# The opening of a fused attention and gated-MLP kernel: tile order, instruction order on four engines, and weight loads in row parts

## Chip, cores, metric

One core of a Trainium2 chip. The metric is the device time in microseconds of one execution; a profile's span is that of TensorE's and the other engines' records, 1.6 to 2.0 us shorter.

## The reference

```python
def _layernorm(x, eps=1e-5):            # over the last axis
    return (x - mean(x)) / sqrt(var(x) + eps)

# A_x [1, 2048, 1024], A_wqkv [1024, 3072], A_wo [1024, 1024], B_w1/B_w3 [1024, 3584], B_w2 [3584, 1024], all bf16
xn = _layernorm(A_x)
q, k, v = split(xn @ A_wqkv)            # 32 heads of 32
s = dilated_window_attention(q, k, v) @ A_wo     # 8 keys per query, 2 apart
g = silu((silu(xn @ B_w1) * (xn @ B_w3)) @ B_w2)
out = A_x + s * g
```

## The kernel before

The rows of x come in four chunks of 512, each of four tiles of 128 rows. Every projection is done with a seven-product (Strassen-like) scheme in bf16 and fp16: "sums" of weight blocks and of x blocks on VectorE, products on TensorE, copies out of the PSUM, the buffer that TensorE writes to, on ScalarE. Below, x1 and x2 are chunks 1 and 2; the "x1 sums" are the sums of blocks of x that chunks 0 and 1 make together. Chunk 0's q, k and v start with two plain products (called `first` and `second` below) that need no sums; the other products of the seven follow when the sums with chunk 1 are there. The parts that the change touches:

```python
x_load(0)                                     # four loads of 256 KB
wq0 = qkv_load(0, 0, slot(2, (4, D)))         # one load of 1 MB: half of the rows of the q weights
wq1 = qkv_load(0, 1, slot(6, (4, D)))
wk0 = qkv_load(1, 0, slot(8, (4, D)))
x_load(1)
...
ln_dve(0, [0])        # statistics and normalising on VectorE, the root on ScalarE
ln_act(0, [1])        # tile 1: two accumulating passes, root and normalising on ScalarE
ln_dve(0, [2])
ln_dve(0, [3])

def p1(g, th):        # first q product, output pair g, half th of the 512 columns
    ...
    act_copy(snap[g][:, :, cols], pf[g][:, :, cols])

spin_in(0, 0, 5)      # idle-filling matmuls: no result, they keep TensorE busy
tpose(0, 0); tpose(0, 1)                      # tile 0: 4 + 4 transposes on TensorE
untp(0, 0, dve_copy); untp(0, 1, sc_copy)     # PSUM -> SBUF
tpose(1, 0); tpose(1, 1)
untp(1, 0, sc_copy); untp(1, 1, sc_copy)
tpose(2, 0); tpose(2, 1)
untp(2, 0, dve_copy)
p1(0, 0)
tpose(3, 0); tpose(3, 1)
...
p1(1, 0); p1(0, 1); p1(1, 1)
...                                           # chunk 1: statistics, 3 tiles transposed by DMA, 1 on TensorE
for t, ... in (q, k, v):
    first_two(...)                            # first and second product of q, k, v
qkv_sums(wq0, wq1, sq)
xn_sums(xT[:, 0], xT[:, 1], b12, xT[:, 2], xs)    # four sums of x blocks, each of 512 columns
qkv_sums(wk0, wk1, sk)
qkv_seven(0, 0, wq0, wq1, sq, None, snap[0:2])
```

A scheduler places the instructions on each engine; `hp()` raises a priority and `tc.issue_after` pins one instruction behind another.

## Time and profile before

| | before |
|---|---|
| time, median of the runs | 725.17 us (724.62 to 725.53, 4 runs) |
| span of the profiled run | 723.4 us |
| TensorE busy | 710.8 us, 98% |
| first q product | 11.42 us |
| seven-product part starts | 33.18 us |

The prediction shows the lines. How to read them: a line of the timeline gives start and duration of a run of like instructions, and in brackets the idle time ahead of it with what ended that. The waits view sums those idle times. For a kernel whose TensorE never idles after its first product, the place to look is the time at which that product starts, and afterwards any mark in the stream (the start of k, of v, of the seven-product part): a mark that moves by 1 us moves the end by 1 us, unless a new hole eats it.

### The profile page before, as it was taken

To read this page: it belongs to the slowest core of one execution; us is meant where nothing else is said; L and a number is where in the kernel's file an instruction comes from. 1 tells how busy PE (TensorE), PEld (TensorE's weight loads), DVE (VectorE), ACT (ScalarE), POOL (GpSimd) and SP (SyncE) were. 2 spreads that over 40 slices of the span, in tenths; PEclk is the share of its full clock that TensorE was granted. 3 is DMA by queue.
4 is the path that set the end of the run, shared out by engine and by line. 5 is a ranking of instruction groups with operands and counts; after the bars stand their busy time and mean duration, and the time that the engine had idled before them with its cause. 6 is when DMAs were issued, how large, how long until landed. Compare 5 with 4: busy or idle time off the path is not lost.

```text
span 723.4 us, 8708 instructions
## 1 busy us (share of the span) xinstructions
PE 710.8 (98%) x3299; PEld 345.6 (48%) x3353; DVE 623.7 (86%) x687; ACT 314.8 (44%) x329; POOL 96.1 (13%) x162
## 2 busy tenths in 40 slices
PE   8999999999999999999999999999999999999996
PEld 5655666554444444444444444444444444444442
DVE  6995879779879878978999999969859989998974
ACT  5754334356545456554545312024454573020233
POOL 0011100011310000233111000000435005000011
PEclk9999999999999999999999999999999999999999
DMA  9966156868755523568756637459799544563615
GB/s 326 278 151 163 58 199 213 270 233 256 230 170 176 174 88 117 160 198 259 247 172 215 204 131 243 150 194 377 172 282 326 156 139 149 163 207 126 211 26 108
DMA packets 119049, 139.51 MB, mean 193 GB/s; under 512 B 17504, under 2 KB 94304, under 8 KB 118368
## 3 DMA queue, kind: packets, MB, share of 16 engines
q1 hardware_dynamic: 104464, 97.01, 43.8%
q0 software_dynamic: 14544, 41.95, 18.5%
q8 instruction: 26, 0.43, 0.2%
q14 instruction: 15, 0.12, 0.1%
HBM read 96.21 MB, written 38.80 MB: 187 GB/s over the span
## 4 chain that ended last, share of the span: by engine, by line
PE 95%; ACT 2%; DVE 1%; issue 1%; DMA 1%; SPq 0%; DVEq 0%; ACTq 0%
PE bm L149 20%; PE am L149 13%; PE em L149 13%; PE db L149 10%; PE bq L149 9%; PE de L149 7%; PE da L149 7%; PE eq L149 5%; PE aq L149 3%; PE af L149 2%; PE wb L149 2%; PE we L149 2%; PE wa L149 2%; DMA wring<-in_A_x_dram 1%; PE af L1022 1%
## 5 line engine op out<-in xcount | busy, mean ns | idle before, releaser
L149 PEld LDWEIGHTS <-wring 128*128 128x128 f16 (+1 forms) x1808 | 185.7, 103 | 205.4 <-issue 1.6
L149 PEld LDWEIGHTS <-h_sb 128*128 128x128 f16 (+1 forms) x1056 | 109.6, 104 | 118.2 <-issue 0.8
L149 PE MATMUL bm<-xs,wring 128*128 128x512 f16 x504 | 117.4, 379 | 0.2
L149 PE MATMUL am<-xT,wring 128*128 128x512 bf16 x322 | 79.0, 379 | 0.8
L149 PE MATMUL db<-wring,h_sb 128*128 128x512 f16 x336 | 73.2, 379 | 0.0
L475 DVE TENSOR_TENSOR BC<-Ep,vT 128x2048 bf16<-128x2048 bf16 x56 | 66.7, 1219 | 0.1
L420 DVE TENSOR_TENSOR pt<-qt,kT 128x4096 bf16<-128x4096 bf16 x24 | 55.0, 2291 | 0.6
L658 DVE TENSOR_TENSOR um<-em,um 128x1024 f32<-128x1024 f32 x28 | 34.2, 1223 | 21.0 <-PE em L149 13.3
L660 ACT ACTIVATE g<-um 128x1024 bf16<-128x1024 f32 x28 | 29.6, 1057 | 48.6 <-DVE um L658 48.6
L149 PE MATMUL da<-wring,h_sb 128*128 128x512 bf16 x219 | 48.7, 379 | 0.3
L461 POOL DMA_DIRECT2D Ep<-pb x64 | 38.0, 601 | 52.2 <-DVE pb L457 46.4
L149 PE MATMUL bm<-h_sb,wring 128*128 128x512 f16 x168 | 39.7, 379 | 0.0
L149 PE MATMUL em<-xs,wring 128*128 128x512 f16 x168 | 39.7, 379 | 0.0
L149 PE MATMUL em<-xT,wring 128*128 128x512 bf16 x161 | 39.2, 379 | 0.3
L485 DVE TENSOR_TENSOR oT<-oT,BC 128x2048 bf16<-128x2048 bf16 x32 | 39.0, 1220 | 0.3
L159 ACT COPY bm<-am 128x1024 f32<-128x1024 f32 x28 | 27.9, 998 | 25.9 <-PE am L149 25.9
L159 ACT COPY pm<-em 128x1024 f32<-128x1024 f32 x28 | 28.4, 1013 | 20.1 <-PE em L149 20.1
L159 ACT COPY um<-bm 128x1024 f32<-128x1024 f32 x28 | 28.4, 1013 | 18.9 <-PE bm L149 18.9
L679 ACT CAST g<-bm 128x1024 bf16<-128x1024 f32 x28 | 28.3, 1010 | 17.4 <-PE bm L149 17.4
L673 DVE TENSOR_TENSOR h_sb<-bm,pm 128x1024 bf16<-128x1024 f32 x21 | 25.6, 1218 | 5.1 <-PE bm L149 5.0
L422 DVE TENSOR_TENSOR pt<-pt 128x2048 bf16<-128x2048 bf16 x24 | 29.3, 1222 | 0.4
L483 DVE TENSOR_TENSOR BC<-BC 128x2048 bf16<-128x2048 bf16 x24 | 29.3, 1221 | 0.4
(202 smaller groups left out, 994.0 us busy)
## 6 DMA issues: line engine op xcount, KB each, us to landing
wring<-in_B_w_dram SPq DMA_DIRECT2D x61, 512.0 KB, 4.5
wring<-t_dram SPq DMA_DIRECT2D x16, 512.0 KB, 3.8
t_dram<-wring POOLq DMA_DIRECT2D x14, 512.0 KB, 4.0
wring<-t_dram SPq DMA_DIRECT2D x16, 384.0 KB, 4.9
wring<-in_B_w_dram SPq DMA_DIRECT2D x12, 384.0 KB, 4.4
wring<-in_A_x_dram SPq DMA_DIRECT2D x16, 256.0 KB, 5.6
Ep<-pb POOLq DMA_DIRECT2D x64, 64.0 KB, 5.4
wring<-in_A_wo_dram SPq DMA_DIRECT2D x8, 512.0 KB, 5.3
```

What stands on the lines that cost most here:

```text
L149: anchor["pe"] = nc.tensor.matmul(ps, lhsT=lhs[k], rhs=rhs[k], start=(first and k == 0), stop=(k == n - 1), skip_group_check=not first,)
L159: nc.scalar.copy(out=out_, in_=in_)
L420: nc.vector.tensor_mul(p_t[:], q[:], kT[:, :, o:o + CH])
L422: nc.vector.tensor_add(p_t[:, 0:4, :], p_t[:, 0:4, :], p_t[:, 4:8, :])
L461: nc.gpsimd.dma_start(out=pr[c][r:P:NR, :, sq * P:(sq + 1) * P], in_=pb[sq * 32:(sq + 1) * 32, :, :])
L475: nc.vector.tensor_mul(dst, E[:, w, :].unsqueeze(1).to_broadcast([P, n, CH]), vT[:, js, o:o + CH])
L483: nc.vector.tensor_add(B, B, C)
L485: nc.vector.tensor_add(A, A, B if w0 else C)
L658: v = nc.vector.tensor_add(su2[:], pe[:], su2[:])
L660: nc.scalar.activation(out=hl["g"][:, :, CH:], in_=su2[:], func=ACTF.Silu)
L673: anchor["v"] = nc.vector.tensor_add(h[:, :, CH:], pb[:], sp5[:])
L679: nc.scalar.copy(out=hl["g"][:, :, 0:CH], in_=pb[:])
```

## The change

Its intent: start the stream of products earlier. Tiles 0 and 1 are normalised first, both by VectorE; the first q products run on tiles 0 and 1 before tiles 2 and 3 are transposed; the q weights come in quarters of 256 KB, taken in the order of their rows; the second half of the k weights and both halves of v come in pieces of 512 KB; and the instructions of the opening on VectorE and ScalarE, and those of TensorE from the k products on, are pinned each behind the one before it. Of chunk 1, TensorE now transposes tile 2, the DMA the other three (before: TensorE tile 3). The first two x1 sums are done for three of four column tiles first, so that they need not wait for the last tile.

```diff
-    wq0 = qkv_load(0, 0, slot(2, (4, D)))
-    wq1 = qkv_load(0, 1, slot(6, (4, D)))
+    wq0 = qkv_load(0, 0, slot(2, (4, D)), 4)
+    wq1 = qkv_load(0, 1, slot(6, (4, D)), 4)
...
-    ln_dve(0, [0])
-    ln_act(0, [1])
-    ln_dve(0, [2])
-    ln_dve(0, [3])
+    st_half(0, 0); st_half(0, 1); st_half(1, 0)
+    st_end(0); root(0)
+    st_half(1, 1); st_end(1); root(1)
+    apply(0); apply(1)
...
+    spin(tpb[0], SP0)              # SP0, SP1 = 2, 1
     tpose(0, 0); tpose(0, 1)
+    with behind("t"):
+        spin(tpb[2], SP1)
     tpose(1, 0); tpose(1, 1)
+    untp(0, 0, sc_copy); untp(1, 0, sc_copy); untp(0, 1, sc_copy)
...                                 # statistics, roots, apply of tiles 2 and 3
+    one = [(k,) for k in range(KH)]
+    p12(0, 0, one, (0,))           # first product, columns 0-255, a weight row part at a time
+    p12(0, 0, one, (1,))
     tpose(2, 0); tpose(2, 1); tpose(3, 0); tpose(3, 1)
...
+    p12(1, 0, one)                 # second product, columns 0-255
+    p12(0, 1, one, (0,)); p12(0, 1, one, (1,))
+    p12(1, 1, [range(KH)])
...                                 # q sums, statistics of chunk 1, k and v products, one by one in order
-    xn_sums(xT[:, 0], xT[:, 1], b12, xT[:, 2], xs)
+    for n, cols in enumerate((slice(0, 3 * P), slice(3 * P, CH))):
+        s_k[n]()
+        dve(nc.vector.tensor_sub, xs[:, 0, :, cols], b12[:, :, cols], xT[:, 0, :, cols])
+        dve(nc.vector.tensor_sub, xs[:, 1, :, cols], xT[:, 2, :, cols], xs[:, 0, :, cols])
+    dve(nc.vector.tensor_sub, xs[:, 2], xT[:, 2], b12)
+    dve(nc.vector.tensor_sub, xs[:, 3], xT[:, 1], xs[:, 1])
```

More of the change, by code (lines that the diff above doesn't have):

```diff
@@ L115 @@
     SLOT = KH * CH
+    SP0, SP1 = 2, 1
     wring = keep.tile([P, 10, SLOT], BF16, name="wring")
@@ L148, in mm @@
         for k in range(n):
-            anchor["pe"] = nc.tensor.matmul(
-                ps, lhsT=lhs[k], rhs=rhs[k], start=(first and k == 0),
-                stop=(k == n - 1), skip_group_check=not first,
-            )
+            with behind("pe") if "open" in anchor else nullcontext():
+                anchor["pe"] = nc.tensor.matmul(
+                    ps, lhsT=lhs[k], rhs=rhs[k], start=(first and k == 0),
+                    stop=(k == n - 1), skip_group_check=not first,
+                )
     def a4(name, shape=(2, CH), dt=FP32):
@@ L165, in flush @@
             pend.pop(0)()
-    def first_two(key, A, b11, b21, snap, e11, mid=lambda: None, pa=None):
-        have, pa = pa, pa or []
-        for g in range(2):
-            if have is None:
-                pa.append(bank2(f"a{key}{g}"))
-                for i in I:
-                    mm(pa[g][:, i], A[g][0][i], b11, True)
-                act_copy(snap[g], pa[g][:])
-        mid()
-        for g in range(2):
-            for i in I:
-                mm(pa[g][:, i], A[g][1][i], b21, False)
-            e11[g](pa[g])
     def seven(key, A, B, e11, e12, e22, e21, snap=None):
@@ L240, in behind, with act, dve @@
         return tc.issue_after(anchor[key].ins) if key in anchor else nullcontext()
+    def act(f, **kw):
+        with hp(), behind("a"):
+            anchor["a"] = f(**kw)
+    def dve(f, *args, **kw):
+        with behind("ln") if "open" in anchor else nullcontext():
+            r = f(*args, **kw)
+        if "open" in anchor:
+            anchor["ln"] = r
     def ln_dve(c, sts):
@@ L307, with qkv_sums @@
     B0 = B_of(xT[:, 0], xT[:, 1], xT[:, 2], xs)
-    def qkv_sums(w0, w1_, st, again=False):
+    def qkv_sums(w0, w1_, st, again=False, parts=False):
         lo = lambda w: w.rearrange("p k (c two j) -> p k c two j", two=2, j=4)[:, :, :, 0]
@@ L323, in qkv_sums @@
             return
-        nc.vector.tensor_add(s1, a21, a22)
-        nc.vector.tensor_sub(s2, s1, a11)
-        nc.vector.tensor_sub(s4, a12, s2)
-        nc.vector.tensor_sub(s3, a11, a21)
+        parts_ = [
+            lambda: dve(nc.vector.tensor_add, s1, a21, a22), lambda: dve(nc.vector.tensor_sub, s2, s1, a11),
+            lambda: dve(nc.vector.tensor_sub, s4, a12, s2), lambda: dve(nc.vector.tensor_sub, s3, a11, a21),
+        ]
         pace["owed"] += 4.5
+        if parts:
+            return parts_
+        for f in parts_:
+            f()
     def qkv_A(w0, w1_, st, g):
@@ L333, in qkv_A @@
         v3 = w0.bitcast(FP16).rearrange("p k (c two j) -> p k two j c", two=2, j=4)
-        sv = [s.rearrange("p k (c j) -> p k j c", j=4) for s in st]
+        sv = [s.rearrange("p k (c j) -> p k j c", j=4) for s in st or ()]
         pick = lambda v, h: [[v[:, k, h, 2 * g + i, :] for k in range(KH)] for i in I]
         sp = lambda q: [[sv[q][:, k, 2 * g + i, :] for k in range(KH)] for i in I]
+        if st is None:
+            return pick(v0, 0), pick(v1, 0)
         return pick(v0, 0), pick(v1, 0), pick(v1, 1), sp(0), sp(1), pick(v3, 1), sp(2)
@@ L375, in qkv_seven, with qkv_load @@
                 mid(g)
-    def qkv_load(t, h, wt):
-        anchor["wq"] = nc.sync.dma_start(out=wt, in_=wqkv_r[:, h * 4:(h + 1) * 4, t * D:(t + 1) * D])
+    def qkv_load(t, h, wt, n=1):
+        for k in range(0, 4, 4 // n):
+            k1 = k + 4 // n
+            anchor["wq"] = nc.sync.dma_start(out=wt[:, k:k1], in_=wqkv_r[:, h * 4 + k:h * 4 + k1, t * D:(t + 1) * D])
         return wt
@@ L984 @@
     wve = [att_tile((4, D), BF16, f"wve{h}") for h in I]
+    wk1 = qkv_load(1, 1, rows(0, 4).rearrange("p (k n) -> p k n", k=4), 2)
+    for h in I:
+        qkv_load(2, h, wve[h][:], 2)
     vsn = att_tile((2, 2, CH), FP32, "vsn")
@@ L991, in tpose @@
     def tpose(st, a):
-        key = a, st // 2
-        if key not in tpb:
-            tpb[key] = bank2(f"tp{a}{st // 2}")
-        tp = tpb[key]
+        if st not in tpb:
+            tpb[st] = bank2(f"tp{st}")
         for k in range(KH):
-            nc.tensor.matmul(
-                tp[:, st % 2, k * P:(k + 1) * P], lhsT=xt[0][:, st, (a * KH + k) * P:(a * KH + k + 1) * P], rhs=ident[:],
+            anchor["t"] = nc.tensor.matmul(
+                tpb[st][:, a, k * P:(k + 1) * P], lhsT=xt[0][:, st, (a * KH + k) * P:(a * KH + k + 1) * P], rhs=ident[:],
                 start=(k == 0), stop=(k == KH - 1), skip_group_check=True,
@@ L1002, in untp @@
     def untp(st, a, eng):
-        with hp():
-            r = eng(out=xT[:, a, :, st * P:(st + 1) * P], in_=tpb[a, st // 2][:, st % 2].rearrange("p (k t) -> p k t", k=KH))
-        if eng == dve_copy:
-            anchor["x"] = r
+        with hp(), behind("a" if eng == sc_copy else "ln"):
+            r = eng(out=xT[:, a, :, st * P:(st + 1) * P], in_=tpb[st][:, a].rearrange("p (k t) -> p k t", k=KH))
+        anchor["ln" if eng == dve_copy else "a"] = r
     dve_copy, sc_copy = nc.vector.tensor_copy, nc.scalar.copy
-    ln_dve(0, [0])
@@ L1010 @@
-    ln_act(0, [1])
-    ln_dve(0, [2])
-    ln_dve(0, [3])
-    pf = {}
-    def p1(g, th):
-        if g not in pf:
-            pf[g] = bank2(f"af0{g}")
-        cols = slice(th * 2 * P, (th + 1) * 2 * P)
-        w = wq0.rearrange("p k (c two j) -> p k two j c", two=2, j=4)
-        for i in I:
-            for k in range(KH):
-                nc.tensor.matmul(
-                    pf[g][:, i, cols], lhsT=w[:, k, 0, 2 * g + i, :], rhs=xT[:, 0, k, cols],
-                    start=(k == 0 and th == 0), stop=(k == KH - 1), skip_group_check=True,
-                )
-        act_copy(snap[g][:, :, cols], pf[g][:, :, cols])
@@ L1028, in spin_in, with st_half @@
-    def spin_in(st, a, n):
-        tpb[a, st // 2] = bank2(f"tp{a}{st // 2}")
-        spin(tpb[a, st // 2], n)
-    spin_in(0, 0, 5)
+    st0 = rows(10, 1, FP32)[:, 0:15 * NST].rearrange("p (a b) -> p a b", b=NST)
+    stats = st0[:, 0:12].rearrange("p a b -> p (a b)").rearrange("p (s h d) -> p s h d", s=NST, h=2)
+    mv = st0[:, 12:14].rearrange("p a b -> p (a b)").rearrange("p (s d) -> p s d", s=NST)
+    rstd = st0[:, 14]
+    def st_half(st, h, c=0):
+        dve(nc.vector.bn_stats, out=stats[:, st, h, :], in_=xt[c][:, st, h * CH:(h + 1) * CH])
@@ new lines, in st_end, with root, apply @@
+    def st_end(st):
+        dve(nc.vector.bn_aggr, out=mv[:, st, :], in_=stats[:, st])
+    def root(st):
+        act(nc.scalar.activation, out=rstd[:, st:st + 1], in_=mv[:, st, 1:2], func=ACTF.Sqrt, bias=eps_t[:], scale=1.0)
+    def apply(st, c=0):
+        r = rstd[:, st:st + 1]
+        dve(nc.vector.reciprocal, out=r, in_=r)
+        dve(
+            nc.vector.tensor_scalar, out=xt[c][:, st, :], in0=xt[c][:, st, :], scalar1=mv[:, st, 0:1], scalar2=r,
+            op0=ALU.subtract, op1=ALU.mult,
+        )
@@ new lines, with p12 @@
+    pf = {}
+    wqs = [w.rearrange("p k (c two j) -> p k two j c", two=2, j=4)[:, :, 0] for w in (wq0, wq1)]
+    def p12(n, th, ks, gs=range(2), save=True):
+        for g in gs:
+            if g not in pf:
+                pf[g] = bank2(f"af0{g}")
+        cols = slice(th * 2 * P, (th + 1) * 2 * P)
+        for kh in ks:
+            for g in gs:
+                for i in I:
+                    for k in kh:
+                        nc.tensor.matmul(
+                            pf[g][:, i, cols], lhsT=wqs[n][:, k, 2 * g + i, :], rhs=xT[:, n, k, cols],
+                            start=(n == 0 and k == 0 and th == 0), stop=(k == KH - 1), skip_group_check=True,
+                        )
+        if n == 0:
+            for g in gs:
+                act(nc.scalar.copy, out=snap[g][:, :, cols], in_=pf[g][:, :, cols])
@@ L1033 @@
+    anchor["open"] = True
+    st_half(0, 0)
+    st_half(0, 1)
+    st_half(1, 0)
+    st_end(0)
+    root(0)
+    st_half(1, 1)
+    st_end(1)
+    root(1)
+    apply(0)
+    apply(1)
+    tpb[0], tpb[1], tpb[2] = [bank2(f"tp{k}") for k in range(3)]
+    spin(tpb[0], SP0)
     tpose(0, 0)
     tpose(0, 1)
-    untp(0, 0, dve_copy)
-    untp(0, 1, sc_copy)
+    with behind("t"):
+        spin(tpb[2], SP1)
     tpose(1, 0)
     tpose(1, 1)
+    untp(0, 0, sc_copy)
     untp(1, 0, sc_copy)
-    untp(1, 1, sc_copy)
+    untp(0, 1, sc_copy)
@@ L1041 @@
+    st_half(2, 0)
+    st_half(2, 1)
+    st_half(3, 0)
+    st_end(2)
+    root(2)
+    st_half(3, 1)
+    st_end(3)
+    untp(1, 1, sc_copy)
+    root(3)
+    apply(2)
+    apply(3)
+    one = [(k,) for k in range(KH)]
+    tpb[3] = bank2("tp3")
+    p12(0, 0, one, (0,))
+    p12(0, 0, one, (1,))
     tpose(2, 0)
     tpose(2, 1)
-    untp(2, 0, dve_copy)
-    p1(0, 0)
     tpose(3, 0)
     tpose(3, 1)
-    untp(3, 0, dve_copy)
-    untp(2, 1, sc_copy)
+    untp(2, 0, sc_copy)
+    untp(2, 1, dve_copy)
@@ L1049 @@
+    untp(3, 0, sc_copy)
     untp(3, 1, dve_copy)
-    p1(1, 0)
-    p1(0, 1)
-    p1(1, 1)
-    wk1 = qkv_load(1, 1, rows(0, 4).rearrange("p (k n) -> p k n", k=4))
+    p12(1, 0, one)
+    p12(0, 1, one, (0,))
+    p12(0, 1, one, (1,))
+    p12(1, 1, [range(KH)])
     sk = rows(4, 6, FP16).rearrange("p (q k n) -> p q k n", q=3, k=4)
     sk = [sk[:, q] for q in range(3)]
-    b12 = rows(12, 2).rearrange("p (k n) -> p k n", k=KH)
-    TPE = (3,)
-    for h in I:
-        qkv_load(2, h, wve[h][:])
@@ L1060 @@
-    for st in range(NST):
-        ln_dve(1, [st])
-        if st not in TPE:
-            for a, d in ((0, b12), (1, xT[:, 2])):
-                nc.sync.dma_start(
-                    out=d[:, :, st * P:(st + 1) * P], in_=xt[1][:, st, a * CH:(a + 1) * CH], transpose=True,
-                )
-    x_load(2)
     sq = rows(20, 6, FP16).rearrange("p (q k n) -> p q k n", q=3, k=4)
     sq = [sq[:, q] for q in range(3)]
-    Bq = B0, B_of(xT1[0], xT1[1], xT1[3], xs1)
-    def tp1(*sts):
-        for st in sts:
-            ln_tp(1, st, [(b12.unsqueeze(1), slice(0, 1)), (xT[:, 2:3], slice(1, 2))])
@@ L1076 @@
-    snap += [vsn[:, 0], vsn[:, 1]]
-    for t, (w0, w1_, ws) in enumerate(((wq0, wq1, sq), (wk0, wk1, sk), (wve[0][:], wve[1][:], sk))):
-        first_two(f"f{t}", [qkv_A(w0, w1_, ws, g) for g in range(2)], B0[0], B0[1],
-                  snap[2 * t:2 * t + 2], [qkv_copy(t, 0, 2 * g) for g in range(2)],
-                  *((lambda: None, [pf[0], pf[1]]), (lambda: None,), (lambda: tp1(*TPE),))[t])
-    with behind("x"):
-        qkv_sums(wq0, wq1, sq)
-    xn_sums(xT[:, 0], xT[:, 1], b12, xT[:, 2], xs)
@@ L1084, with first, second @@
-    qkv_sums(wk0, wk1, sk)
+    b12 = rows(12, 2).rearrange("p (k n) -> p k n", k=KH)
+    ws = [(wq0, wq1), (wk0, wk1), (wve[0][:], wve[1][:])]
+    snap += [vsn[:, 0], vsn[:, 1]]
+    def first(t, g):
+        pf[t, g] = bank2(f"af{t}{g}")
+        for i in I:
+            mm(pf[t, g][:, i], qkv_A(*ws[t], None, g)[0][i], B0[0], True)
+        act(nc.scalar.copy, out=snap[2 * t + g], in_=pf[t, g][:])
+    def second(t, g):
+        for i in I:
+            mm(pf[t, g][:, i], qkv_A(*ws[t], None, g)[1][i], B0[1], False)
@@ new lines, in store, with mean_var, flip @@
+    def store(t, g):
+        act(nc.scalar.copy, out=qkv_dst(t, 0, 2 * g)[0], in_=pf[t, g][:])
+    def mean_var(st):
+        st_half(st, 0, 1)
+        st_half(st, 1, 1)
+        st_end(st)
+    def flip(st, eng):
+        cols = slice(st * P, (st + 1) * P)
+        dst = b12[:, :, cols], xT[:, 2, :, cols]
+        if eng == "dma":
+            for a in I:
+                anchor["tr1"] = nc.sync.dma_start(out=dst[a], in_=xt[1][:, st, a * CH:(a + 1) * CH], transpose=True)
+            return
+        tp = bank2(f"tq{st}")
+        for k in range(KT):
+            with behind("pe"):
+                anchor["pe"] = nc.tensor.matmul(
+                    tp[:, k // KH, (k % KH) * P:(k % KH + 1) * P], lhsT=xt[1][:, st, k * P:(k + 1) * P], rhs=ident[:],
+                    start=(k % KH == 0), stop=(k % KH == KH - 1), skip_group_check=True,
+                )
+        for a in I:
+            act(nc.scalar.copy, out=dst[a], in_=tp[:, a].rearrange("p (k t) -> p k t", k=KH))
@@ new lines @@
+    pf[0, 0], pf[0, 1] = pf[0], pf[1]
+    s_q = qkv_sums(wq0, wq1, sq, parts=True)
+    s_q[0]()
+    s_q[1]()
+    s_q[2]()
+    store(0, 0)
+    store(0, 1)
+    mean_var(0)
+    root(0)
+    first(1, 0)
+    mean_var(1)
+    root(1)
+    apply(0, 1)
+    flip(0, "dma")
+    first(1, 1)
+    mean_var(2)
+    apply(1, 1)
+    flip(1, "dma")
+    root(2)
+    second(1, 0)
+    store(1, 0)
+    second(1, 1)
+    mean_var(3)
+    apply(2, 1)
+    root(3)
+    store(1, 1)
+    s_q[3]()
+    apply(3, 1)
@@ new lines @@
+    flip(3, "dma")
+    first(2, 0)
+    flip(2, "pe")
+    first(2, 1)
+    for g in range(2):
+        second(2, g)
+    for g in range(2):
+        store(2, g)
+    with behind("tr1"):
+        x_load(2)
+    Bq = B0, B_of(xT1[0], xT1[1], xT1[3], xs1)
+    s_k = qkv_sums(wk0, wk1, sk, parts=True)
+    for n, cols in enumerate((slice(0, 3 * P), slice(3 * P, CH))):
+        s_k[n]()
+        dve(nc.vector.tensor_sub, xs[:, 0, :, cols], b12[:, :, cols], xT[:, 0, :, cols])
+        dve(nc.vector.tensor_sub, xs[:, 1, :, cols], xT[:, 2, :, cols], xs[:, 0, :, cols])
@@ L1085 @@
+    dve(nc.vector.tensor_sub, xs[:, 2], xT[:, 2], b12)
+    dve(nc.vector.tensor_sub, xs[:, 3], xT[:, 1], xs[:, 1])
+    anchor.pop("open")
+    with behind("ln"):
+        s_k[2]()
+        s_k[3]()
     qkv_seven(0, 0, wq0, wq1, sq, None, snap[0:2])
-    x_load(3)
+    with behind("tr1"):
+        x_load(3)
     def tr(c):
```

## The prediction

> **What bounds the kernel now.** I read the page's engine table first, then the waits of TensorE over the whole run, then the timelines of the four engines for the first 35 us, because the change touches nothing later than that, and last the DMA issues with their landings.
>
> ```profile
> PE 710.8 (98%) x3299; PEld 345.6 (48%) x3353; DVE 623.7 (86%) x687; ACT 314.8 (44%) x329; POOL 96.1 (13%) x162
> PE 95%; ACT 2%; DVE 1%; issue 1%; DMA 1%; SPq 0%; DVEq 0%; ACTq 0%
> ```
>
> TensorE carries 95% of the chain that ended last. Its waits in the whole run are four:
>
> ```profile
> PE tp L997 <- DVE wring L256: 1.5, 2, 1.3
> PE warm L141 <- DVE warm L138: 1.3, 1, 1.3
> PE tp L997 <- ACT xT L1004: 0.3, 1, 0.3
> PE tp L997 <- ACT wring L276: 0.2, 1, 0.2
> ```
>
> The same question asked from 11.4 us to the end gives an empty answer. So from its first product on TensorE streams to the end without a hole; the time can fall only by starting that stream earlier, or by doing less in it. The timeline of TensorE (start, duration) shows the beginning:
>
> ```profile
> 1.29 4.97 PE L141 MATMUL warm<-warm 128*128 128x512 bf16 x12 [1.29 <-DVE warm L138]
> 6.09 1.24 PE L141 MATMUL tp<-warm 128*128 128x512 bf16 x5
> 7.57 0.62 PE L997 MATMUL tp<-ident,wring 128*128 128x128 bf16 x8 [0.23 <-DVE wring L256]
> 9.47 0.62 PE L997 MATMUL tp<-ident,wring 128*128 128x128 bf16 x8 [1.28 <-DVE wring L256]
> 10.29 0.40 PE L997 MATMUL tp<-ident,wring 128*128 128x128 bf16 x4 [0.20 <-ACT wring L276]
> 10.94 0.39 PE L997 MATMUL tp<-ident,wring 128*128 128x128 bf16 x4 [0.25 <-ACT xT L1004]
> 11.42 1.03 PE L1022 MATMUL af<-xT,wring 128*128 128x256 bf16 x8
> 12.29 0.61 PE L997 MATMUL tp<-ident,wring 128*128 128x128 bf16 x8
> 12.74 2.79 PE L1022 MATMUL af<-xT,wring 128*128 128x256 bf16 x24
> 15.37 7.07 PE L149 MATMUL af<-xT,wring 128*128 128x512 bf16 x31
> 22.27 3.71 PE L149 MATMUL af<-xT,h_sb 128*128 128x512 bf16 x16
> ```
>
> The x tiles are transposed as the normalisation delivers them; the first q product starts at 11.42 and the q work ends about 15.37 + 16 x 0.216 = 18.82 us (the two groups from 15.37 to 22.27 are 32 matmuls, one record is missing: 6.90 / 32 = 0.216 us). That 18.82 is the mark to compare with. The reason that it starts so late: tile 1 is normalised by ScalarE (two accumulating passes, a root, one more pass from 8.99 to 10.23), and VectorE takes tile 2 before it.
>
> The weights matter as well. Issue records of the q, k and v loads and landing times, first of the load issued at 2.67, then of the second half of the k weights issued at 9.41:
>
> ```profile
> wring<-in_A_wqkv_dram SPq DMA_DIRECT2D x1, 1024.0 KB, 7.7
> h_sb<-in_A_wqkv_dram SPq DMA_DIRECT2D x1, 1024.0 KB, 12.0
> ```
>
> Half of the q weights is complete at 2.67 + 7.7 = 10.4 us. The landing records of the same trace give 13.1 for the other half, 15.8 and 21.4 for the halves of k, 24.2 and 26.8 for v: 2.7 us for each MB. The DMA share is 0.99 to 1.06 from 7.5 to 33 us. Moving the compute earlier moves none of these bytes.
>
> **What the Trainium skill says.** "DMA: Bandwidth & Descriptors", section "Queues, rings and completion order": a copy is split over up to 16 rings, each taking descriptors in order, and one engine's progress says nothing about the others'; only the full count means landed. The trace agrees: the sixteen increments of that first q half come between 8.1 and 10.4 us, two late ones apart all by 9.1. So four quarters in place of one load finish early except the last, which waits for the same slow engine. "TensorE: Matmul & The Clock Gate", section "Back-to-back issue gap": N/2.4 + 2.5 ns when warm, so 109 ns for 256 columns and 216 for 512. The trace agrees: 24 products of 256 columns fill 12.74 to 15.37, 110 ns each. Cutting a product into column halves is therefore nearly free. The same page, section "What's actually happening", puts the warm-up at some 3.4 us of activity; here twelve 512-column matmuls take 4.97 us, five later ones 1.24, and products after a 1.3 us hole still run warm, so shorter holes should not cool it.
>
> **The change part by part.**
>
> *Normalisation.* ScalarE's passes over tile 1 (1.06 + 1.13 + 1.24 us and small ones) go; VectorE does tiles 0 and 1 as a pair. From its rows: tile 0 lands at 3.3, tile 1 at 4.18; half a statistic has a pitch of 0.6, an aggregation 0.1 to 0.2, a root on ScalarE 0.3, a normalising pass 0.45 (0.53 to its end). So: three halves and an aggregation 3.32 to 5.4, last half and aggregation to 6.2, tile 0 normalised at 6.8 (before 7.51), tile 1 at 7.3 (before 10.23). Transposes at 6.85 to 7.4 and, after one filler matmul, 7.6 to 8.1. Spinning ends at 6.6, so it holds nothing up.
>
> *First product.* ScalarE copies out in the order that the product needs: two copies at a pitch of 0.51, the second beginning when tile 1's half is there (8.05) and ending 8.65. The first product may start at 8.65 in place of 11.42, a gain of 2.8 us so far.
>
> *Weights.* It takes the q half by row quarters. Quarters 0 to 2 I estimate at 7.5, 8.5 and 9.4, the fourth at 10.4, from the 6.4 at which the last x tile lands and the 10.4 above. The order is one output pair through all four quarters, then the other. So the first pair ends at 10.4 + 2 x 0.109 = 10.6, the second at 11.5. 16 products would have ended at 8.65 + 1.75 = 10.4: the weights take back 1.1 us.
>
> *The rest of q.* Tiles 2 and 3 are normalised by 10.5 and 11.1 and their 16 transposes stand behind the products: 11.5 to 12.55. Then 48 products of 256 columns at 0.1095: 12.55 to 17.8. The other q half lands at 13.1 and its last quarter is wanted at 13.9; ScalarE's copy of tile 3 ends at 13.3 and is wanted at 14.3. So q ends at 17.8, against 18.82: **1.0 us gained**. TensorE's added work is 32 x 0.1095 - 16 x 0.216 = 0.05 us, included.
>
> *The k and v weights.* k starts at 17.8 (its first half is there at 15.8) and the second half is wanted at 21.25, its later quarter at 21.7, against a landing at 21.4. Just in time, through the cut in two. v is wanted at 24.7 and 28.6, there at 24.2 and 26.8. So this caps the gain at some 1.3 us.
>
> *VectorE and the x1 sums.* From 14.0: three q sums of 1.15, four tiles of statistics and passes, the fourth sum, the first k sum; I get the first column part of xs at 28.0 (the ScalarE copy of tile 2 is its wait), the last part at 31.2, the second sum at 32.2. Before, the seven-product part starts at 33.18 and its first sum ended 32.2. Now it starts at 32.1: margin 0.9, and the next one is wanted at 33.8: margin 1.6. Splitting by columns takes tile 3, the last to be flipped by DMA, out of three quarters of the work. Those transposes end at 29.9 by the 2.5 us landing of the last ones before. So nothing here should reach TensorE.
>
> *Everything after* has the same products and waits. The end, 711.8 to 723.4, is ScalarE and VectorE work that moves along.
>
> Sum: 2.77 for the earlier first product, less 1.1 for the weights, less 0.5 because 16 transposes lie behind the first product where before only 8 did (0.065 each), less 0.05 for the halves and some 0.1 of small waits: 1.0 to 1.1. 725.15 - 1.05 = **724.1 us**.
>
> **The rivals.** (1) The stream starts some 2 us earlier as designed and keeps all of it: the quarters land evenly by 9.5. For it speaks that the fast engines had their shares by 8.1; against it that a full count is needed. It would give 723.1 to 723.5, and then the second k half at 21.4 would show as a new wait. (2) The hand order makes the engines wait on each other: VectorE's fixed order puts a statistic of x2 between the two last sums, and root calls stand behind copies on ScalarE. If the sums come a microsecond later than I have, TensorE gets a hole before the seven-product part and the result is 724.8 to 725.5. My margin of 0.9 after 28 us of stacked estimates is thin. (3) Weights are the bound throughout and quarters land later than one big load, as each has its own completion: the gain is 0 to 0.4 us. The bytes in their order are the same, so I doubt it.
>
> **Range and chances.** Runs of before lie within 0.6 us. The q weights' last quarter may be 0.7 us off in either direction, the k landing caps the upside. 8 in 10: **723.3 to 724.9**. Two per cent is 14.5 us, more than the whole beginning: faster by over 2% 0.005, within 2% **0.99**, slower 0.005.
>
> **What would show it.** First product near 8.7, with waits on the q weight load of 0.5 to 1.2 us among TensorE's waits; tile 2's transposes at about 11.5; k at 17.8 and v at 24.7; seven-product part at about 32.1 with no wait; from there the same stream shifted by 1 us. It is wrong if the first k or x1 sum shows as a new wait, or the q weights don't show at all.

## The result

723.93 us median (723.55 to 724.26, 4 runs) against 725.17 (724.62 to 725.53, 4 runs). The ratio is 0.9983, interval 0.9966 to 1.0001. By the 2% rule the two are the same; the gain is 1.2 us by the medians, 1.6 us by the spans of the two profiled runs (721.8 against 723.4). The interval includes 1; that of the second run of the changed kernel, below, does not.

First a line of the changed kernel's page, busy time of each engine, then its waits of TensorE over the whole run (engine, line, released by: us, times, longest):

```profile
PE 710.0 (98%) x3313; PEld 346.2 (48%) x3367; DVE 624.9 (87%) x690; ACT 312.9 (43%) x326; POOL 95.7 (13%) x162
```

```profile
PE warm L142 <- DVE warm L139: 1.3, 1, 1.3
PE af L1049 <- ACT xT L1011: 0.7, 1, 0.7
PE tp L1004 <- DVE wring L236: 0.5, 1, 0.5
```

No line names the q weights. The timeline of TensorE answers to the one of before:

```profile
6.76 0.62 PE L1004 MATMUL tp<-ident,wring 128*128 128x128 bf16 x8 [0.51 <-DVE wring L236]
7.44 0.61 PE L1004 MATMUL tp<-ident,wring 128*128 128x128 bf16 x8
8.72 1.91 PE L1049 MATMUL af<-xT,wring 128*128 128x256 bf16 x16 [0.67 <-ACT xT L1011]
10.72 1.27 PE L1004 MATMUL tp<-ident,wring 128*128 128x128 bf16 x16
11.83 5.41 PE L1049 MATMUL af<-xT,wring 128*128 128x256 bf16 x48
17.08 3.62 PE L151 MATMUL af<-xT,wring 128*128 128x512 bf16 x15
20.53 3.62 PE L151 MATMUL af<-xT,h_sb 128*128 128x512 bf16 x16
31.34 1.89 PE L151 MATMUL eq<-xs,h_sb 128*128 128x512 f16 x8
33.33 1.89 PE L151 MATMUL bq<-xs,h_sb 128*128 128x512 f16 x8
```

Behind the earlier first product stands the normalisation of tile 1, on ScalarE before (first line, ready at 10.23) and on VectorE now (second line, ready at 7.36):

```profile
8.99 1.24 ACT L276 ACTIVATE wring<-wring,v 128x1024 bf16<-128x1024 bf16 x1 [1.04 <-DVE v L273]
6.81 0.55 DVE L236 TENSOR_SCALAR wring<-wring,h_sb 128x1024 bf16<-128x1024 bf16 x1
```

The lead over the kernel before, mark by mark: the first product 2.70 us (11.42 to 8.72); the end of q 1.74 us (18.82 to 17.08), since 16 transposes instead of 8 lie behind the first product, with waits of 0.2 us for tile 2 and 0.2 us for tile 3; the second k products 1.74 (22.27 to 20.53); the seven-product part 1.84 (33.18 to 31.34); its second product 1.58 (34.91 to 33.33). The last step is a new hole: eight matmuls from 31.34 on end their stream at 31.34 + 8 x 0.216 = 33.07, and the next starts at 33.33. From there the lead of 1.6 us stays to the end. What made the hole is seen in the timeline of VectorE of the changed kernel:

```profile
30.51 0.42 DVE L236 TENSOR_TENSOR xs<-h_sb,xT 128x512 f16<-128x512 bf16 x1
32.17 0.69 DVE L248 BATCH_NORM_STATS2 stats<-wring 128x6 f32<-128x512 bf16 x1 [1.24 <-DMA wring<-in_A_x_dram]
32.78 0.41 DVE L236 TENSOR_TENSOR xs<-xT,xs 128x512 f16<-128x512 bf16 x1
```

A statistic of the next x chunk stands between the last parts of the two x1 sums and waits 1.24 us for its load, while the sum behind it, which needs nothing but a result of 30.9, ends at 33.2. That fits the 33.33; the second run of this kernel, below, also names the sum as what TensorE waited for.

### The profile page after: what moved, and what is told of

The parts are those of the page before. It is cut to its first block, busy times and chain, and to the rows that moved or that the text cites. A ratio compares the mean times of both kernels' runs of the same rounds, so it can differ in the third digit from the quotient of the medians.

```text
span 721.8 us, 8746 instructions
## 1 busy us (share of the span) xinstructions
PE 710.0 (98%) x3313; PEld 346.2 (48%) x3367; DVE 624.9 (87%) x690; ACT 312.9 (43%) x326; POOL 95.7 (13%) x162
## 4 chain that ended last, share of the span: by engine, by line
PE 95%; ACT 2%; DVE 2%; issue 1%; DMA 0%; DVEq 0%; ACTq 0%
PE bm L151 20%; PE am L151 13%; PE em L151 13%; PE db L151 10%; PE bq L151 9%; PE de L151 7%; PE da L151 7%; PE eq L151 5%; PE aq L151 3%; PE wb L151 2%; PE af L151 2%; PE we L151 2%; PE wa L151 2%; DVE h_sb L236 1%; PE af L1049 1%
## 5 line engine op out<-in xcount | busy, mean ns | idle before, releaser
L151 PEld LDWEIGHTS <-wring 128*128 128x128 f16 (+1 forms) x1792 | 183.4, 102 | 204.3 <-issue 2.2
```

The source lines that it names most:

```text
L151: anchor["pe"] = nc.tensor.matmul(ps, lhsT=lhs[k], rhs=rhs[k], start=(first and k == 0), stop=(k == n - 1), skip_group_check=not first,)
```

## The experiments

Theories at the start. A load counts as landed when the last of its sixteen completions has come; "straggler" means that one or two of them come late, as in the first half of the q weights before, complete at 10.4 us with fourteen of sixteen there by 9.1. A: the straggler comes from loading the half in one piece. B: it comes and goes by run. For the hole at 33.1: the x2 statistic, or something else. A third pair of theories (C and D) came from the third run.

**The changed kernel again.** No edit.

> The changed kernel once more, unchanged, to learn how much of its opening is the same in a second run. Theory A (the q weights land without a straggling engine because they are loaded in quarters): the four quarters complete near 6.6, 7.6, 8.3 and 9.0 us as in the first run, the 16 first products run 8.7 to 10.5 with no wait, q ends at about 17.1, ratio to before 0.997 to 0.999. Theory B (the straggler comes and goes by run): the quarters may end as late as 10.4 and the first product then waits about 1 us.

724.01 us median (723.91 to 724.64, 5 runs), ratio to before 0.9973 (0.9961 to 0.9985) on a chip where before had 726.21 (724.7 to 726.9, 11 runs). This time the weights do show in the waits of TensorE:

```profile
PE af L1049 <- DMA wring<-in_A_wqkv_dram: 0.2, 1, 0.2
PE bq L151 <- DVE xs L236: 0.2, 1, 0.2
```

The landing records give 8.1, 8.8, 9.4 and 10.1 us for the quarters; in the first run they were 6.5, 7.6, 8.2 and 8.9. So the straggler is there with quarters too (the first quarter's last completion came 0.65 us after the fifteenth). The wait for the quarters cost little: the 48 products behind the transposes start 3.16 us after the first product, against 3.11 in the first run. The hole behind the x1 sum is there again.

**The q weights in two whole loads.**

```diff
-    wq0 = qkv_load(0, 0, slot(2, (4, D)), 4)
-    wq1 = qkv_load(0, 1, slot(6, (4, D)), 4)
+    wq0 = qkv_load(0, 0, slot(2, (4, D)))
+    wq1 = qkv_load(0, 1, slot(6, (4, D)))
```

> The changed kernel with each half of the q weights loaded in one piece, as before. Theory A (one big load makes a few DMA engines straggle): the first half completes at about 10.4 us as in the kernel before, the first product starts there instead of 8.7, q ends at about 18.8, and the time is that of before within 0.3 us. Theory B (the straggler is chance, the total of bytes decides): the half completes at about 9.0, the first product starts 0.3 us later than in the changed kernel, and the time is within 0.4 us of the changed kernel's, 723.9 to 724.3.

723.57 us median (723.21 to 725.93, 6 runs), ratio 0.9972 (0.9958 to 0.9986). The run of 725.93 lies 1.9 us above the next and has a clock of 0.996 against 0.998 and 0.999 in the others. The whole half completed at 9.0 us and the first product started at 9.01. From the waits of TensorE in this kernel:

```profile
PE af L1049 <- DMA wring<-in_A_wqkv_dram: 0.8, 1, 0.8
```

Hardly any of that 0.8 us is lost, as in the changed kernel TensorE waits 0.7 at the same place for ScalarE's copy (first product at 8.72): the 48 products start at 11.99 instead of 11.83, and the first transposes already 0.16 us later (6.92 against 6.76). So theory A falls: a whole load can land without a straggler, quarters can land with one. B stands. In the timed runs the quarters gain nothing that shows.

**The kernel before with the q weights in quarters.**

```diff
-    def qkv_load(t, h, wt):
+    def qkv_load(t, h, wt, n=1):      # as in the change
-    wq0 = qkv_load(0, 0, slot(2, (4, D)))
+    wq0 = qkv_load(0, 0, slot(2, (4, D)), 4)      # and wq1
```

> The kernel before with only the q weights loaded in quarters. Its first product waits for the copies of ScalarE, not for the weights, so both theories expect the first product at 11.4 us and the same time as before within 0.3 us (ratio 0.9995 to 1.0005). Theory A expects the last quarter of the first half at about 9 us, theory B anything from 9.0 to 10.4.

725.22 us median (724.64 to 727.15, 5 runs), ratio 0.999 (0.9976 to 1.0004): no gain that shows, as expected. But the profiled run was the one of 727.15, and its first product started at 11.83, only 0.4 us later than in the first profile of before. The rest is in its view of stretches of 3.41 us, laid along the moments at which the trace's record of the clock changes (columns: stretch and its length, TensorE's busy time and instructions, granted clock, DMA share, GB/s):

```profile
8.71:12.12 3.41, 1.69 (x19) 1.00 1.05 404
12.12:15.54 3.42, 3.42 (x22) 0.50 1.05 387
15.54:18.95 3.41, 3.36 (x26) 1.00 1.06 389
```

The clock of TensorE was halved from 12.1 to 15.5 us, just as the products ran, after a stretch in which TensorE had been busy for 1.7 of 3.4 us. Half a clock for 3.4 us costs 1.7 us. On this chip five of eleven runs of before lie at 726.6 to 726.9 and the others at 724.7 to 726.2; four of the five have a granted clock of 0.995, none of the others one under 0.997. (Two slower runs of before don't fit: 726.21 here and 726.30 on another chip have a clock of 0.999.) This gave theory C, that the holes of an opening let the clock fall in some executions, and D, that such drops are chance.

**The statistics of x2 behind the x1 sums.**

```diff
-    tr(2)
+    with behind("ln"):
+        tr(2)
```

> The changed kernel with the statistics of x2 ordered behind the last of the x1 sums. Reason on trial: the 1.24 us wait of VectorE for the x2 tile, standing ahead of the last part of the second x1 sum, made TensorE idle 0.27 us at 33.1 us. If so the sum's last part ends at about 31.3 instead of 33.2, the hole is gone, the second product of the seven starts at 33.07, and the time is 0.27 us less than the changed kernel's in the same rounds. Rival: the next sum or a later buffer takes the place of the wait and the time is unchanged within 0.1 us.

723.53 us median (723.48 to 723.96, 5 runs), ratio 0.9965 (0.9953 to 0.9977), beside 724.01 of the changed kernel in the same rounds. The timeline of VectorE in this kernel now has

```profile
30.81 0.42 DVE L236 TENSOR_TENSOR xs<-h_sb,xT 128x512 f16<-128x512 bf16 x1
31.26 0.42 DVE L236 TENSOR_TENSOR xs<-xT,xs 128x512 f16<-128x512 bf16 x1
```

and TensorE goes from one product to the next in 1.73 us for eight matmuls, without a hole:

```profile
31.47 1.89 PE L151 MATMUL eq<-xs,h_sb 128*128 128x512 f16 x8
33.20 1.89 PE L151 MATMUL bq<-xs,h_sb 128*128 128x512 f16 x8
```

Expected was 0.27 us; the medians differ by 0.48, the means by 0.57 (724.17 and 723.60). The profiled run of the changed kernel on this chip also waited 0.2 us each for q and k weights, which may be part of the difference. The cause of the hole is shown: the edit moves the statistics and nothing else, and the hole is gone. The times of this version lie below those of both kernels, by 0.5 and 2.7 us in the medians on this chip, which the 2% rule still calls the same; the 2.7 has the slow executions of before in it.

**The kernel before with its first hole filled.**

```diff
     tpose(0, 0)
     tpose(0, 1)
...
+    tpb[0, 1] = bank2("tp01")
+    with behind("t"):
+        spin(tpb[0, 1], 5)
     tpose(1, 0)
```

> The kernel before with five idle-filling matmuls on TensorE after the transposes of the first x tile, and nothing else of the change. Theory C (the runs of before at 726.6 to 726.9 us are those in which the clock of TensorE was halved for one window of 3.4 us because the opening left it idle too long): the filled kernel has no such run, all its runs lie at 724.6 to 726.2, its profile shows no stretch at half clock, while of the runs of before on this chip a third or more lie at 726.5 and over. Rival D (the clock drop is chance and has nothing to do with the holes): the filled kernel shows it as often as before.

725.30 us median (724.79 to 725.88, 5 runs), ratio 0.9995 (0.9983 to 1.0008). No run of it at 726.5 or over, but on this chip only one of nine runs of before was (726.76, clock 0.995), not a third. In keeping with C, and too few slow ones to tell it from D.

**Tile 1 normalised by ScalarE again.**

```diff
-    st_half(1, 0)
     st_end(0)
     root(0)
-    st_half(1, 1)
-    st_end(1)
-    root(1)
+    with hp():
+        ln_act(0, [1])
     apply(0)
-    apply(1)
```

> The changed kernel with x tile 1 normalised by ScalarE again (its discarded pass output put in a free row), to undo the part of the change that pairs tiles 0 and 1 on VectorE. By the durations of the profile tile 1 is ready near 9.4 us, the first product starts near 10.5 instead of 8.7, q ends at about 18.5 instead of 17.1 and the time is 1.2 to 1.6 us more than the changed kernel's. Rival: if the weights or the later tiles bound the opening, the time changes by less than 0.5 us.

726.32 us median (725.04 to 726.48, 5 runs), ratio to before 1.0007 (0.9993 to 1.0021). In its profiled run (725.04) the pairing's worth is seen: the first product at 10.86 instead of 8.72, the end of q at 18.75 instead of 17.08, and a span of 723.3 against 721.8. Its first product, and from its waits of TensorE:

```profile
10.86 1.91 PE L1049 MATMUL af<-xT,wring 128*128 128x256 bf16 x16 [0.67 <-ACT xT L1011]
```

```profile
PE tp L1004 <- ACT wring L274: 1.8, 1, 1.8
```

So without VectorE's pair nothing is left of the change's gain (the two faster runs, 725.04 and 725.34, lie among those of before). The pair is needed for the gain; whether it would bring it alone, in the old order of products and loads, was not run. The times fall in two groups, 725.0 to 725.3 and 726.3 to 726.5.

**The x1 sums in one piece**, with the statistics behind them.

```diff
-    for n, cols in enumerate((slice(0, 3 * P), slice(3 * P, CH))):
-        s_k[n]()
+    for cols in (slice(0, CH),):
+        s_k[0]()
+        s_k[1]()
```

> As the run with the x2 statistics behind the sums, but the first two x1 sums in one piece instead of two column parts. If the parts are needed, the first sum ends after 31.5 us, TensorE shows a wait ahead of the seven-product part and the time is 0.2 to 1 us over that of the run with the parts. If tile 3's transposes land near 28.9 and 30.1 as its issue times and 2.4 us say, the sums end at about 30.1 and 31.4, which is earlier than in parts, and the time is the same within 0.15 us.

724.39 us median (724.34 to 724.73, 5 runs), ratio 0.9984 (0.9971 to 0.9996). The sums ended near 30.3 and 31.6 and the seven-product part started at 31.55 without a wait, as the transposes' landings said. The loss is elsewhere, as its waits of TensorE show:

```profile
PE bq L151 <- ACT bq L161: 0.8, 1, 0.8
```

The scheduler had put ScalarE's first root of x2, which waits for VectorE, ahead of a copy that TensorE needs at 40.2 us. So this run doesn't tell the parts' worth; a later one does.

**Both findings: whole q loads and the statistics behind the sums.**

```diff
+    wq0 = qkv_load(0, 0, slot(2, (4, D)))      # and wq1, as above
+    with behind("ln"):
+        tr(2)
```

> The changed kernel with both findings: the x2 statistics behind the x1 sums, and the q weights in two whole loads. If the quarters gain nothing by themselves, it is within 0.2 us of the run with the statistics moved alone (723.5 us), and 0.3 to 0.6 us less than the changed kernel. If the quarters pay, it is 0.2 to 0.4 us slower than that run, from a wait of the first product on the weights.

724.11 us median (723.24 to 724.32, 5 runs), ratio 0.9976 (0.9964 to 0.9989). The profiled run (724.11) had the straggler: the half completed at 10.2 us, and the waits of TensorE have

```profile
PE af L1049 <- DMA wring<-in_A_wqkv_dram: 1.9, 1, 1.9
```

with the seven-product part at 32.43 instead of 31.47. This is what quarters can save: with the last quarter at 10.1 the changed kernel waited 0.2 us at this place, with the whole load 1.2 us longer than for ScalarE's copy (the first product at 10.22 instead of 9.0). Some 0.8 us of that reached the later marks, since the transposes behind the first products had less to wait for: against the run with the statistics alone the 48 products start 0.96 us later, and the first transposes 0.19. That is one trace; over the timed runs no gain of the quarters shows. The chip was another than that of the run with the statistics alone, so the medians of the two aren't compared.

**Filled and unfilled opening with tile 1 on ScalarE, on one chip.** The filled one has nine idle-filling matmuls instead of one between the transposes of tiles 0 and 1.

```diff
-    SP0, SP1 = 2, 1
+    SP0, SP1 = 2, 9
```

> The kernel of the run with tile 1 on ScalarE, its hole of 1.8 us on TensorE filled with eight more idle matmuls. Theory C (holes in the opening let the clock be halved for a window of 3.4 us in some executions): all five runs lie near 725.0 to 725.5, none at 726.3 or over, and none has a stretch at half clock. Rival D (the drop is chance): two or three of five lie at 726.3 to 726.5 as in the unfilled one.

> The unfilled kernel with tile 1 on ScalarE once more, on the same chip as the filled one. Theory C: again one to four of five runs are 1.2 to 1.7 us above the others, with a granted clock of 0.995 to 0.997. Rival D: as many as in the filled kernel.

Filled: 725.15 us median (724.82 to 725.29, 5 runs), ratio 0.9996 (0.9983 to 1.0009), granted clock 0.998 to 0.999 in each. Unfilled, median 725.9, ratio 1.0011 (0.9997 to 1.0026): 727.86, 724.87, 727.75, 725.08, 725.15, 726.65, with a clock of 0.993 in the two slowest. The profiled run of the unfilled one is that of 727.86; its view of stretches (same columns as above) has two such windows:

```profile
6.07:9.49 3.42, 1.42 (x13) 1.00 1.01 367
9.49:12.90 3.41, 2.32 (x15) 0.50 1.04 398
12.90:16.31 3.41, 3.41 (x24) 0.50 1.06 390
16.31:19.73 3.42, 3.42 (x36) 1.00 1.05 387
```

Its 16 first products took 3.57 us instead of 1.91. With the two runs of this kernel together, six of eleven lie 1.0 us or more above the others of their session; of the two filled kernels none of ten, but one of these is a filling of the kernel before, on a chip where before itself was rarely slow. On this one chip it is three of six against none of five, which would come by chance in 12% of draws (56 of the 462 ways to pick five of eleven runs avoid the three slow ones). The faster runs of unfilled (724.87 to 725.15) lie within those of filled, so the fill costs nothing that shows. C is supported by this and two traces but not shown against D; that every slow run of before was such a drop is inferred from its clock and time, as only these traces were taken.

**The x1 sums in one piece, with the statistics behind them and the copy ahead of the root.**

```diff
+    with hp():
+        anchor["cp"] = nc.scalar.copy(...)     # the copy that fills the next product's bank
...
+    with behind("cp"):
         nc.scalar.activation(out=rstd[:], ..., func=ACTF.Sqrt, ...)
```

> The x1 sums in one piece, statistics of x2 behind them, and ScalarE's first root of x2 held behind the copy that TensorE waited for in the earlier run with whole sums. If the parts are not needed by themselves, the 0.78 us wait at 41 us is gone, no wait ahead of the seven-product part shows, and the time is that of the run with parts on this chip within 0.15 us. If they are needed, it is 0.2 us or more slower.

**The statistics behind the sums, again, as its reference.** No new edit.

> The changed kernel with the statistics of x2 behind the sums, once more, as the reference of the whole-sums run on this chip: 723.4 to 724.0 us, ratio to before 0.996 to 0.998, no run at half clock.

Whole sums: 723.46 us median (723.24 to 723.51, 5 runs). In parts: 723.38 (723.26 to 723.57, 5 runs). Both 0.9972 of before (0.996 to 0.9984). The wait at 41 us is gone, the seven-product part starts at 31.63 and 31.56. So the column parts aren't needed once the statistics stand behind the sums. The best kernel is the one with the statistics behind the sums, in parts or whole: in parts 0.5 us under the changed kernel where the two ran on one chip (the fourth run).

## Why the prediction was right or wrong

The time was right: 723.93 against 724.1, within 723.3 to 724.9. That it is so close is partly luck, as the sum below shows. By the prediction's own signs the account of the weights was wrong: it called itself wrong if the q weights don't show at all among TensorE's waits, which happened in the first run, or if an x1 sum shows as a new wait, which happened in the second (0.2 us). Its steps, one by one:

- *Normalisation and first product*: first product foretold at 8.65, measured 8.72; transposes at 6.85 and 7.6, measured 6.76 and 7.44. The run with tile 1 back on ScalarE shows that without this part no gain is left.
- *Weights take back 1.1 us*: this term was mis-sized. TensorE's wait for the quarters measured 0 in the first profiled run and 0.2 in two others, with 0.05 us or less of it left at the 48 products; it was 1.2 us only with whole loads and a straggler. The step that failed is taking one run's 10.4 us for a fixed landing time; in the nine traces of the changed kernel and its variants with loads in quarters the last quarter landed between 8.9 and 10.1 us, and in the four traces with whole loads the half landed between 9.0 and 10.4. The prediction's own rival 1 had "the quarters land evenly", which is what the profiled run showed.
- *The rest of q*: 17.8 foretold, 17.08 measured: the 1.1 of the weights, less 0.07 for the later first product and some 0.3 for transposes that waited for the normalisation of tiles 2 and 3; in the prediction the wait for the weights would have covered that. 48 products at 0.1095 us took 5.25, exactly as said. (The skill's section that the prediction names for this spacing, "Back-to-back issue gap" of "TensorE: Matmul & The Clock Gate", means its formula for single products and gives about 131 ns for 512 columns in a stream; here 16 of them in a stream, from 17.08 to 20.53, took 216 ns each, as the formula says.)
- *The k weights cap the gain at 1.3 us*: not seen in the profiled run, where the lead was 1.74 at that place; the k weights landed at 19.2 and 20.4 there, not 21.4 (with a straggler of 1.3 us: fifteen completions of the first part were there by 17.9). In the second run of the changed kernel they landed at 20.2 and 21.4, the latter as foretold, and did cost some 0.2 us.
- *"Nothing here should reach TensorE"*: wrong by some 0.26 us. Rival 2 had named the statistic between the two last sums; I took its margin of 1.6 us as enough and left out that its x2 load is issued only behind the last transposes, at 28.9.
- *"Shorter holes should not cool it"*: right as far as seen for the changed kernel, whose two profiles show no halved clock in the opening (its nine runs have a mean clock of 0.997 or more), and wrong as a rule: in the run of before with quarters no single hole was longer than 1.3 us, yet the clock was halved; and the changed kernel with whole loads had one run of 725.93 at 0.996. It hardly touched the first comparison, where no run of before was slow, but on another chip, with five of eleven runs of before slow, the same kernel had 0.9973 instead of 0.9983.
- *Readings*: "runs of before lie within 0.6 us" was too narrow: 0.9 us in this comparison, 2.5 over all chips. The DMA share of 0.99 to 1.06 up to 33 us is a mean over long stretches; the parts from 25.3 to 26.7 and from 30 to 31 us show 0.36 and 0.35.

So the total was right with errors of opposite sign: 1.1 us for the weights that mostly weren't lost, against some 0.3 us of waits for tiles 2 and 3 and a hole of 0.3 us that it hadn't counted (the first profiled pair differs by 1.6, the medians by 1.2). The mechanism, an earlier start of a nearly unbroken stream that then keeps most of its lead, was right.

## What to carry to other kernels

Where one engine streams to the end, look for gains at its first real instruction and follow the lead from mark to mark; a fixed order on another engine should not put an instruction that waits for a late load ahead of one that the bound engine needs. A landing time from one trace is one draw: look at several before a term is built on it. Loads cut in parts, so that a late one costs only its last part, cost nothing that shows here and would by the estimate above have saved some 0.8 us in one trace. Here four stretches of 3.4 us had TensorE busy for only 1.4 to 1.8 us; two of them (1.42, 1.69) were followed by a halved clock, two (1.61, 1.83) not. So where the holes of an opening add up to that much, a fill is worth a try, judged by several executions, as only some show the cost.

## What the Trainium skill lacked or had wrong

- "TensorE: Matmul & The Clock Gate", section "What's actually happening", has the clock halved after one or more idle windows of about 3.4 us. Here it was halved after windows in which TensorE was busy 1.4 and 1.7 of 3.41 us by the profile, so the window need not be idle; one with 1.6 in another execution (of 725.04 us) and one with 1.8 had no drop, so the limit is not sharp in these terms. Another section of the page, "A second HAM failure mode: psum-queue depth-cycling", tells of short idle times between groups of matmuls that make the clock swing, without a measure of how much idling it takes. The length of the window (3.41 us, once two of them in a row) and the factor of a half agree with the page.
- "DMA: Bandwidth & Descriptors", section "Why a DMA increments its semaphore by 16 and not by 1", says that the engines of one copy finish independently and that only the full count means landed; it gives no size for the spread. Here the first and last of sixteen completions of a 1 MB load lay 0.8 us apart in one run (8.2 to 9.0) and 2.3 us in another (8.1 to 10.4). In the latter run the lag stayed with the later loads up to the first half of v (21.7 to 24.2), but not with its second half (26.7 to 26.8).
- No page says how far equal executions of one kernel differ: before, 724.4 to 726.9 us in 31 runs on three chips.
